# Gated mix of an SSM and a two-layer feed-forward: the narrow tail blocks of both layers are regrouped, and two x tiles are loaded earlier

## The chip, the cores and the metric

The kernel runs on one core of a Trainium2 chip, as one launch. The metric is the device time in microseconds of an execution; 214.89 us is the median of six executions of the kernel before (214.46 to 215.27). All times below are microseconds unless marked ns.

## The reference

For 2048 tokens of width 640, one input x goes through two branches, and a gate of each token mixes them. Cut to what matters:

```
g = sigmoid((x * gate_w).sum(-1))                 # one number per token

# branch A: a diagonal complex recurrence over the tokens
Bu = einsum("bld,pd->blp", x, B_bar)              # 640 -> 640 complex
for t in range(L):  h = Lam_bar * h + Bu[:, t]
a = 2 * einsum("blp,dp->bld", hseq, Cmat).real + x * Dskip

# branch B: feed-forward
h = gelu(x @ w1 + b1)                             # 640 -> 1728
b = h @ w2 + b2                                   # 1728 -> 640

out = g * a + (1 - g) * b
```

The width 1728 is 13 blocks of 128 and a last one of 64. The 64 are what is called the tail here: in the first layer they are 64 output columns, in the second layer 64 rows of the sum.

## The kernel before

**Tiling.** Tokens are taken in four quarters of 512 (index q), each of two SSM blocks of 256 (b) and four chunks of 128 (c). xT[q] holds x transposed, features on partitions. For each quarter:

- `m1(q)` (L633): 13 blocks of the first layer, five matmuls of 512 tokens each (L640), gelu by ScalarE into Gl[q % 2] (L647).
- `bproj(q)` (L672): the projection to the recurrence's input, real and imaginary, ten blocks of five matmuls (L680); ScalarE moves them to U (L689).
- `ssm(b)` (L694): VectorE alone. It rotates U (pre), scans along the tokens (L720, scan), and rotates back (post) into H[b % 3], reading and writing the tiles V and W on the way.
- `gates(q)` (L593): VectorE sums x * gate_w from the untransposed tile xn[q % 2] (L597), ScalarE takes tanh (L604), VectorE makes the factors g and 1 - g.

Output is made by chunks of 128 tokens in `outs` (L872). `m2_prime` (L747) has ScalarE write the bias b2 into two banks of PSUM, one for each half of the 640 columns (L754). `m2_main` (L758) adds 13 matmuls to each half (L767). `m2_tails` (L774) adds the 64 tail rows (L781): for the first half they are read from partitions 0 to 63, for the second from 64 to 127, so the two matmuls use two row tiles of the array, and the gelu values of the tail and W2's tail rows have to stand in both halves of the partitions. `m2_out` (L788) has ScalarE scale the sum by 1 - g into E1 (L795). `cproj` (L802) makes branch A's output from H and CT, 20 matmuls over two banks (L815), which ScalarE scales by g into E2 (L826). `comb` (L830) has VectorE compute xg = x * g * Dskip (L834) and add xg, E1 and E2 (two additions through the helper at L481) into osb, which SP stores (L868). E1, E2, osb and H have three buffers each, xg and xn two. For the last chunk, VectorE adds the second half straight out of PSUM (L848).

The first layer's tail, `m1_tail(q)` (L651), takes two quarters at once: ten matmuls of 64 columns each, alternately on the two column halves of the array, into the lower and upper 64 partitions of one bank (L658). Four gelus follow (L667), since the result of each quarter is written twice, to partitions 0 to 63 and to 64 to 127 of the last block of Gl.

**The order of the work.** There are eight banks of PSUM, given out in turn by `next_bank` (L589) as the program is written. Each operation is declared with what it reads and writes, a length in a cost model and a priority; a list planner (L43) then fixes the order on each engine before the program is emitted. TensorE's priority is the order of declaration, so its queue follows the program's text where the model finds the operands ready. On ScalarE evictions of outputs (5) come before the bias writes (8), and these before gelus and U (10). On VectorE the combination (-50) comes before everything else of the steady state, xg is at 90 + 20q, and pre, scan and post of block b at 100, 101 and 102 + 10b. SP issues the loads by the numbers at their calls: the x tile of quarter 1 at 32, W2 and b2 at 33 to 34.4, the transposed C at 36 and 37, dsk at 38, the second xn at 38.2, and the x tiles of quarters 2 and 3 last, at 39 and 40 (L579, L580). POOL loads the later xn tiles (`xnload`) when the chunks that use the old ones are through.

The text of the order is at L883 to L911. The first tail group, `m1_tail(0)`, comes after m1(1); the second, `m1_tail(2)`, after m1(3). The chunks go through `outs` in groups of 2, 2, 2, 2, 3, 3 and 2, each group with one `m2_tails`, and within a chunk cproj follows m2 directly.

Of the kernel before, what the change touches and what calls it, by code (L numbers as in the profile page):

```python
# [9 lines left out]
BF16 = mybir.dt.bfloat16  # L10
I32 = mybir.dt.int32
ACT = mybir.ActivationFunctionType
# [135 lines left out]
class Prog:  # L148
# [8 lines left out]
    def op(self, name, eng, dur, reads, writes, fn, prio=None, lat=0.0, after=()):  # L157
        deps = {}
        for k in reads:
            for w in self.last_w.get(k, ()):  # L160
                deps[w.idx] = w
        for k in writes:
            for w in self.last_w.get(k, ()):
                deps[w.idx] = w
            for r in self.last_r.get(k, ()):
                deps[r.idx] = r
        for a in after:
            deps[a.idx] = a
        deps = list(deps.values())
        E = self.E  # L170

        def run(eg, deps=deps, eng=eng, fn=fn):
            E.wait(eng, *[d.done for d in deps if not (eng == "pe" and d.eng == "pe")])
            return fn()

        it = self.sch.add(name, eng, dur, deps, run, prio=prio, lat=lat)
        for k in writes:
            self.last_w[k] = [it]
            self.last_r[k] = []
        for k in reads:  # L180
            self.last_r.setdefault(k, []).append(it)
        return it


def bass_gated_mix__ssm_conv_s5__dense_activation_gelu__prompt_kernel(
# [18 lines left out]
    _, S, D = A_x.shape  # L204
# [3 lines left out]
    KD = D // 128  # L208
    KP = P // 128
    NQ = S // 512  # L210
    NCH = S // 128
    T = 256
    NB = S // T
    NF = (F + 127) // 128
    FL = F - (NF - 1) * 128
    assert FL <= 64
    HALF = D // 2
# [8 lines left out]
    with ExitStack() as es:  # L226

        def SB(name, shape, dt):
            return es.enter_context(nc.sbuf_tensor(name, list(shape), dt))
# [4 lines left out]
        W2sb = SB("W2sb", [128, NF, D], BF16)  # L234
        BT = SB("BT", [128, 2, KD, P], BF16)
        CT = SB("CT", [128, 2, KP, D], BF16)
        Gl = [SB(f"Gl_{i}", [128, NF, 512], BF16) for i in range(2)]
        dsk = SB("dsk", [128, D], BF16)
        gwb = SB("gwb", [128, D], BF16)
        b2b = SB("b2b", [128, D], BF16)  # L240
# [3 lines left out]
        b1col = cols[:, 3 * KP:3 * KP + NF]  # L244
# [42 lines left out]
        PS = [es.enter_context(nc.psum_tensor(f"ps{i}", [128, 512], FP32)) for i in range(8)]  # L287
# [13 lines left out]
        op = pr.op  # L301

        def inc(eng, ins):
            return E.inc(eng, ins, eng + "_s")

        def dma_inc(eng, ins, sem):
            SEM(sem)
            E.count.setdefault(sem, 0)
            ins.then_inc(sems[sem], 16)
            E.count[sem] += 16  # L310
            return (sem, E.count[sem])

        def d_act(n):
            return 0.26 + n * 0.00084
# [4 lines left out]
        def d_mm(n):  # L319
            return n / 2400.0 + 0.004  # L320


        def load(name, eng, sem, dst, src, writes, prio, dur=0.5, lat=2.5, reads=(), **kw):
            def fn():
                return dma_inc(eng, engines[eng].dma_start(dst, src), sem)  # L325
            return op(name, eng, dur, reads, writes, fn, prio=prio, lat=lat)
# [18 lines left out]
        def xtrans(q, ks, prio, dur):  # L345
            load_T(f"xT{q}_{ks[0]}", f"l_xT{q}_{ks[0]}", [(xT[q][:, ks[0]:ks[-1] + 1, :], x2[q * 512:(q + 1) * 512, ks[0] * 128:(ks[-1] + 1) * 128])],
                   [("xT", q, k) for k in ks], prio, dur)
# [57 lines left out]
        for i, (k, c0, c1) in enumerate(((0, 0, 2), (0, 2, 4), (1, 0, 4))):  # L405
            bank = 7 - i
# [169 lines left out]
            load_T(f"C{ci}", f"l_C{ci}", [(CT[:, ci, :, :], src)], [("CT", ci)], prio=36 + ci, dur=4.1)  # L576
        load("dsk", "sp", "l_dsk", dsk[:, :], A_Dskip.partition_broadcast(128), ["dsk"], prio=38)
        xnload(1, "sp", prio=38.2)
        xtrans(2, range(KD), 39, 3.4)  # L579
        xtrans(3, range(KD), 40, 3.4)  # L580

        ctr = {"bank": 0, "pe": 0}

        def pe_prio():
            ctr["pe"] += 1
            return ctr["pe"]


        def next_bank():  # L589
            ctr["bank"] += 1  # L590
            return (ctr["bank"] - 1) % 8
# [41 lines left out]
        def m1(q, j0=0):  # L633
            for jf in range(j0, NF - 1):
# [13 lines left out]

                op(f"ge_{q}_{jf}", "act", d_act(512), [("bank", bank), "b1col"], [("gl", q % 2, jf)], f_ge, prio=10)

        def m1_tail(q):  # L651
            bank = next_bank()

            def f_mm():
                t = None
                for k in range(KD):
                    for i in range(2):
                        t = nc.tensor.matmul(PS[bank][64 * i:64 * i + FL, :], W1sb[:, k, nmain:F], xT[q + i][:, k, :],  # L658
                                             start=(k == 0), stop=(k == KD - 1))
                return inc("pe", t)  # L660

            op(f"m1t_{q}", "pe", KD * d_mm(512) + 0.25, XT[q] + XT[q + 1] + [("w1", "r", 1)], [("bank", bank)], f_mm, prio=pe_prio())
            for i in range(2):
                for u in range(2):

                    def f_ge(i=i, u=u):
                        return inc("act", nc.scalar.activation(Gl[i][64 * u:64 * u + FL, NF - 1, :], PS[bank][64 * i:64 * i + FL, :], ACT.Gelu_apprx_tanh,  # L667
                                                               bias=b1col[64 * i:64 * i + FL, NF - 1:NF]))

                    op(f"get_{q}_{i}{u}", "act", d_act(512), [("bank", bank), "b1col"], [("gt", i, u)], f_ge, prio=10)  # L670

        def bproj(q):  # L672
            for ci in range(2):
# [71 lines left out]
        mbank = {}  # L745
# [28 lines left out]
        def m2_tails(cs):  # L774
            def f_mm():
                t = None
                for c in cs:
                    q, t4 = c // 4, c % 4
                    for hf in range(2):
                        r = slice(64 * hf, 64 * hf + FL)  # L780
                        t = nc.tensor.matmul(PS[mbank[c, hf]][:, 0:HALF], Gl[q % 2][r, NF - 1, t4 * 128:(t4 + 1) * 128],  # L781
                                             W2sb[r, NF - 1, hf * HALF:(hf + 1) * HALF], start=False, stop=False, skip_group_check=True)
                return inc("pe", t)

            op(f"m2t_{cs[0]}", "pe", len(cs) * d_mm(HALF) + 0.2, [("gt", c // 4 % 2, u) for c in cs for u in range(2)] + ["w2b", "w2c"],
               [("bank", mbank[c, hf]) for c in cs for hf in range(2)], f_mm, prio=pe_prio())

        def m2_out(c):  # L788
# [13 lines left out]
        def cproj(c):  # L802
            q, b, s = c // 4, c // 2, c % 2
            for hf in range(2):
                bank = next_bank()
                cbank[hf] = bank
                cols = CCOLS[hf] if c == NCH - 1 else slice(hf * HALF, (hf + 1) * HALF)
                n = cols.stop - cols.start

                def f_mm(bank=bank, cols=cols, n=n):  # L810
                    t = None
                    i = 0
                    for ci in range(2):
                        for k in range(KP):
                            t = nc.tensor.matmul(PS[bank][:, 0:n], H[b % NHB][:, ci, k, s * 128:(s + 1) * 128], CT[:, ci, k, cols],  # L815
                                                 start=(i == 0), stop=(i == 2 * KP - 1))
                            i += 1
                    return inc("pe", t)

                op(f"c_{c}_{hf}", "pe", 2 * KP * d_mm(n), [("H", b % NHB), ("CT", 0), ("CT", 1)], [("bank", bank)], f_mm, prio=pe_prio())  # L820

                if c == NCH - 1:
                    continue

                def f_ev(bank=bank, cols=cols):
                    return inc("act", nc.scalar.activation(E2[c % NE][:, cols], PS[bank][:, 0:HALF], ACT.Copy, scale=gcol[:, c:c + 1]))  # L826

                op(f"e2_{c}_{hf}", "act", d_act(HALF), [("bank", bank), ("g", q)], [("E2", c % NE, hf)], f_ev, prio=5)
# [40 lines left out]

            op(f"st{c}", "sp", 0.5, [("osb", c % NO, 0), ("osb", c % NO, 1)], [], f_st, prio=1000 + c, lat=2.5)  # L870

        def outs(*cs):  # L872
            for c in cs:
                m2_prime(c)
            for c in cs:
                m2_main(c)
                if c == cs[0]:
                    m2_tails(cs)
                m2_out(c)
                cproj(c)  # L880
                comb(c)

        m1_first()  # L883
        m1(0, NW)
# [1 line left out]
        ssm(0)  # L886
        gates(0)
        m1(1)
        m1_tail(0)
        ssm(1)  # L890
        bproj(1)
        ssm(2)
        gates(1)
        outs(0, 1)
        outs(2, 3)
        for q in range(2, NQ):
            ssm(2 * q - 1)
            bproj(q)
            ssm(2 * q)
            m1(q)  # L900
            if q % 2 == 1:
                m1_tail(q - 1)
            xnload(q, "pool")
            gates(q)
            if q < NQ - 1:
                outs(4 * q - 4, 4 * q - 3)
                outs(4 * q - 2, 4 * q - 1)
        outs(NCH - 8, NCH - 7, NCH - 6)
        ssm(2 * NQ - 1)
        outs(NCH - 5, NCH - 4, NCH - 3)  # L910
        outs(NCH - 2, NCH - 1)  # L911

        order = pr.sch.order()
        ptr = {e: 0 for e in order}
# [57 lines left out]
```

## Time and profile before

| What | Value |
|---|---|
| Median of six runs | 214.89 (214.46 to 215.27) |
| The profiled execution | 214.74 |
| Its span, first to last instruction | 213.4 |
| Granted TensorE clock | 1.00 |
| TensorE on the chain that ended last, from / to | 7.71 / 211.31 |
| L767, second layer: 416 matmuls of 128x320 | 59.1 busy |
| L781, its tails: 32 matmuls on 64 rows | 3.4 busy |
| L658, first layer's tails: 20 matmuls on 64 columns | 2.5 busy |
| L667, gelus of the tails: 8 | 5.5 busy, 683 ns each |
| L754, bias into PSUM: 32 | 14.1 busy, 441 ns each |

A page of the profile gives the busy time of each engine (PE is TensorE's matmuls, PEld its weight loads, which run beside them, DVE VectorE, ACT ScalarE, SP the queue that issues DMAs), the chain of work that ended last, and groups of instructions by line. Neighbouring matmuls overlap in the array and their ends are modelled, so the busy times of single groups of matmuls add up to more or less than the time they take; the chain in order of time is better for that, since it counts each stretch once. An idle time is shown with what ended it, as in [1.37 <-ACT E L826]: 1.37 us, ended by ScalarE's write at line 826.

### The profile page before, as it was taken

To read this page: it belongs to the slowest core of one execution; us is meant where nothing else is said; L and a number is where in the kernel's file an instruction comes from. 1 tells how busy PE (TensorE), PEld (TensorE's weight loads), DVE (VectorE), ACT (ScalarE), POOL (GpSimd) and SP (SyncE) were. 2 spreads that over 40 slices of the span, in tenths; PEclk is the share of its full clock that TensorE was granted. 3 is DMA by queue.
4 is the path that set the end of the run, shared out by engine and by line. 5 is a ranking of instruction groups with operands and counts; after the bars stand their busy time and mean duration, and the time that the engine had idled before them with its cause. 6 is when DMAs were issued, how large, how long until landed. Compare 5 with 4: busy or idle time off the path is not lost.

```text
span 213.4 us, 3114 instructions
## 1 busy us (share of the span) xinstructions
PE 209.9 (98%) x1264; PEld 119.7 (56%) x1264; DVE 188.7 (88%) x262; ACT 113.3 (53%) x205; POOL 2.5 (1%) x10
## 2 busy tenths in 40 slices
PE   8999999999999999999999999999999999999996
PEld 3344444444567675444467767444446777677673
DVE  2499999999899999999999959999999998988712
ACT  2489556679554234557835332556786554535230
POOL 1000000000000010000000010000000000000000
DMA  5999899698000040000000013000000010001000
GB/s 145 309 261 196 218 383 202 159 235 141 0 0 34 31 125 31 31 0 0 0 3 0 31 45 144 15 16 0 3 0 2 0 34 31 31 3 61 31 34 31
DMA packets 31114, 16.08 MB, mean 75 GB/s; under 512 B 22908, under 2 KB 30332, under 8 KB 31100
## 3 DMA queue, kind: packets, MB, share of 16 engines
q1 hardware_dynamic: 30752, 14.57, 27.4%
q0 software_dynamic: 288, 1.31, 2.0%
q8 instruction: 10, 0.16, 0.3%
q14 instruction: 4, 0.03, 0.0%
q10 hardware_dynamic: 60, 0.01, 0.0%
HBM read 7.63 MB, written 2.62 MB: 48 GB/s over the span
## 4 chain that ended last, share of the span: by engine, by line
PE 95%; DMA 2%; ACTq 1%; POOL 0%; issue 0%; DVE 0%; POOLq 0%
PE ps L767 27%; PE ps L640 22%; PE ps L815 21%; PE ps L680 20%; PE ps L620 3%; DMA rows<-in_B_b_dram 2%; PE ps L781 1%; PE ps L658 1%; ACTq L325 1%; DVE osb L848 0%; POOL io_i L381 0%; PE ps L431 0%; POOL rows L371 0%; POOL st_i L383 0%; POOL st_i L382 0%
## 5 line engine op out<-in xcount | busy, mean ns | idle before, releaser
L767 PE MATMUL ps<-W2sb,Gl 128*128 128x320 bf16 x416 | 59.1, 299 | 0.0
L767 PEld LDWEIGHTS ps<-W2sb,Gl 128*128 128x128 bf16 x416 | 40.6, 98 | 16.5 <-ACT Gl L647 0.4
L640 PE MATMUL ps<-xT,W1sb 128*128 128x512 bf16 x220 | 48.1, 379 | 0.0
L815 PE MATMUL ps<-CT,H 128*128 128x320 bf16 (+2 forms) x320 | 46.1, 299 | 0.0
L720 DVE TENSOR_TENSOR_SCAN W<-atab,V 128x1280 bf16<-128x1280 f32 x16 | 44.3, 2812 | 0.3
L680 PE MATMUL ps<-xT,BT 128*128 128x512 bf16 x200 | 43.8, 379 | 0.0
L815 PEld LDWEIGHTS ps<-CT,H 128*128 128x128 bf16 x320 | 30.7, 98 | 13.5 <-issue 1.6
L795 ACT ACTIVATE E<-ps,g1col 128x320 bf16<-128x320 f32 x32 | 16.1, 526 | 40.5 <-PE ps L781 21.5
L640 PEld LDWEIGHTS ps<-xT,W1sb 128*128 128x128 bf16 x220 | 21.5, 98 | 26.0
L647 ACT ACTIVATE Gl<-ps,cols 128x512 bf16<-128x512 f32 x44 | 29.7, 690 | 11.5 <-PE ps L640 11.5
L680 PEld LDWEIGHTS ps<-xT,BT 128*128 128x128 bf16 x200 | 19.5, 98 | 23.4 <-ACT Gl L647 0.4
L689 ACT ACTIVATE U<-ps 128x512 bf16<-128x512 f32 x40 | 23.6, 595 | 15.7 <-PE ps L680 15.7
L826 ACT ACTIVATE E<-ps,gcol 128x320 bf16<-128x320 f32 x30 | 15.8, 528 | 17.9 <-PE ps L815 17.9
L754 ACT ACTIVATE ps<-b2b 128x320 f32<-128x320 bf16 x32 | 14.1, 441 | 1.0
L834 DVE SCALAR_TENSOR_TENSOR xg<-xn,gcol,dsk 128x640 bf16<-128x640 bf16 x16 | 13.8, 882 | 0.3
L481 DVE TENSOR_TENSOR osb<-xg,E 128x640 bf16<-128x640 bf16 x15 | 7.3, 486 | 7.7 <-ACT E L826 7.6
L597 DVE SCALAR_TENSOR_TENSOR scr<-xn,gwb 128x640 bf16<-128x640 bf16 x16 | 13.2, 823 | 0.4
L481 DVE TENSOR_TENSOR V<-V,W 128x1280 bf16<-128x1280 bf16 x16 | 12.5, 822 | 0.3
L481 DVE TENSOR_TENSOR H<-H,V 128x1280 bf16<-128x1280 bf16 x16 | 12.5, 822 | 0.3
L481 DVE TENSOR_TENSOR V<-mr,U 128x2560 bf16<-128x2560 bf16 x8 | 11.9, 1489 | 0.2
L481 DVE TENSOR_TENSOR H<-c,W 128x2560 bf16<-128x2560 bf16 x8 | 11.9, 1488 | 0.1
L481 DVE TENSOR_TENSOR V<-s,W 128x2560 bf16<-128x2560 bf16 x8 | 11.9, 1485 | 0.0
(79 smaller groups left out, 102.1 us busy)
## 6 DMA issues: line engine op xcount, KB each, us to landing
out_dram<-osb SPq DMA_DIRECT2D x15, 160.0 KB, 1.8
W2sb<-in_B_w_dram SPq DMA_DIRECT2D x1, 2080.0 KB, 11.1
xn<-in_A_x_dram POOLq DMA_DIRECT2D x2, 640.0 KB, 4.7
W1sb<-in_B_w_dram SPq DMA_DIRECT2D x4, 256.0 KB, 4.1
xn<-in_A_x_dram SPq DMA_DIRECT2D x1, 640.0 KB, 7.5
W1sb<-in_B_w_dram SPq DMA_DIRECT2D x1, 480.0 KB, 4.8
W1sb<-in_B_w_dram SPq DMA_DIRECT2D x1, 400.0 KB, 5.6
xn<-in_A_x_dram SPq DMA_DIRECT2D x1, 384.0 KB, 5.6
```

Source lines behind the costliest of these rows:

```text
L481: return inc("dve", nc.vector.tensor_tensor(out=o, in0=a, in1=b, op=o_))
L640: t = nc.tensor.matmul(PS[bank][:, :], W1sb[:, k, jf * 128:(jf + 1) * 128], xT[q][:, k, :], start=(k == 0), stop=(k == KD - 1))
L647: return inc("act", nc.scalar.activation(Gl[q % 2][:, jf, :], PS[bank][:, :], ACT.Gelu_apprx_tanh, bias=b1col[:, jf:jf + 1]))
L680: t = nc.tensor.matmul(PS[bank][:, :], BT[:, ci, kd, k * 128:(k + 1) * 128], xT[q][:, kd, :], start=(kd == 0), stop=(kd == KD - 1))
L689: return inc("act", nc.scalar.activation(dst, src, ACT.Copy, scale=1.0 if ci == 0 else -1.0))
L720: t = inc("dve", nc.vector.tensor_tensor_scan(out=g[:, ci, :], data0=a, data1=v[:, ci, :], initial=0.0, op0=ALU.mult, op1=ALU.add))
L754: return inc("act", nc.scalar.activation(PS[bank][:, 0:HALF], b2b[:, cols], ACT.Copy))
L767: t = nc.tensor.matmul(PS[bank][:, 0:HALF], Gl[q % 2][:, jf, t4 * 128:(t4 + 1) * 128], W2sb[:, jf, cols], start=False, stop=False, skip_gr ...
L795: return inc("act", nc.scalar.activation(E1[c % NE][:, cols], PS[bank][:, 0:HALF], ACT.Copy, scale=g1col[:, c:c + 1]))
L815: t = nc.tensor.matmul(PS[bank][:, 0:n], H[b % NHB][:, ci, k, s * 128:(s + 1) * 128], CT[:, ci, k, cols], start=(i == 0), stop=(i == 2 * K ...
L826: return inc("act", nc.scalar.activation(E2[c % NE][:, cols], PS[bank][:, 0:HALF], ACT.Copy, scale=gcol[:, c:c + 1]))
L834: return inc("dve", nc.vector.scalar_tensor_tensor(out=xg[c % 2][:, :], in0=xn[q % 2][:, c % 4, :], scalar=gcol[:, c:c + 1], in1=dsk[:, :] ...
```

## The change

1. The gelu values of the tail leave Gl and get four tiles of their own, Gt, one per quarter. ScalarE writes each once, to partitions 0 to 63; a DMA on SP copies it to partitions 64 to 127.
2. Both calls of `m1_tail` stand together after m1(1), so the tails of all tokens are made there, from the x tiles of all four quarters.
3. The x tiles of quarters 2 and 3 move in SP's order from the end of the loads to a place before W2 (priorities 32.6 and 32.7).
4. `outs` takes the four chunks of a quarter as one group: eight banks are primed with the bias, one `m2_tails` of eight matmuls follows the first chunk's m2, and cproj and comb of a chunk come after the m2 of the next one. The last block's `ssm` is declared inside the third group, after chunk 9's cproj, which is the last reader of the H buffer that it writes.

```diff
-        Gl = [SB(f"Gl_{i}", [128, NF, 512], BF16) for i in range(2)]
+        Gl = [SB(f"Gl_{i}", [128, NF - 1, 512], BF16) for i in range(2)]
+        Gt = [SB(f"Gt_{i}", [128, 512], BF16) for i in range(NQ)]
...
-        xtrans(2, range(KD), 39, 3.4)
-        xtrans(3, range(KD), 40, 3.4)
+        xtrans(2, range(KD), 32.6, 3.4)
+        xtrans(3, range(KD), 32.7, 3.4)
...
             for i in range(2):
-                for u in range(2):
-
-                    def f_ge(i=i, u=u):
-                        return inc("act", nc.scalar.activation(Gl[i][64 * u:64 * u + FL, NF - 1, :], PS[bank][64 * i:64 * i + FL, :], ACT.Gelu_apprx_tanh,
-                                                               bias=b1col[64 * i:64 * i + FL, NF - 1:NF]))
-
-                    op(f"get_{q}_{i}{u}", "act", d_act(512), [("bank", bank), "b1col"], [("gt", i, u)], f_ge, prio=10)
+
+                def f_ge(i=i):
+                    return inc("act", nc.scalar.activation(Gt[q + i][0:FL, :], PS[bank][64 * i:64 * i + FL, :], ACT.Gelu_apprx_tanh,
+                                                           bias=b1col[64 * i:64 * i + FL, NF - 1:NF]))
+
+                op(f"get_{q}_{i}", "act", d_act(512), [("bank", bank), "b1col"], [("gt", q + i, 0)], f_ge, prio=10)
+                load(f"gt{q + i}", "sp", f"l_gt{q + i}", Gt[q + i][64:64 + FL, :], Gt[q + i][0:FL, :], [("gt", q + i, 1)], 500, lat=2.5, reads=[("gt", q + i, 0)])
...
-                        t = nc.tensor.matmul(PS[mbank[c, hf]][:, 0:HALF], Gl[q % 2][r, NF - 1, t4 * 128:(t4 + 1) * 128],
+                        t = nc.tensor.matmul(PS[mbank[c, hf]][:, 0:HALF], Gt[q][r, t4 * 128:(t4 + 1) * 128],
...
-        def outs(*cs):
+        def outs(q, mid=None):
+            cs = range(4 * q, 4 * q + 4)
             for c in cs:
                 m2_prime(c)
             for c in cs:
                 m2_main(c)
                 if c == cs[0]:
                     m2_tails(cs)
                 m2_out(c)
-                cproj(c)
-                comb(c)
+                if c > cs[0]:
+                    cproj(c - 1)
+                    comb(c - 1)
+                    if mid is not None and c == cs[0] + 2:
+                        mid()
+            cproj(cs[-1])
+            comb(cs[-1])
...
-        m1_tail(0)
+        for q in range(0, NQ, 2):
+            m1_tail(q)
         ssm(1)
         bproj(1)
         ssm(2)
         gates(1)
-        outs(0, 1)
-        outs(2, 3)
+        outs(0)
         for q in range(2, NQ):
...
             m1(q)
-            if q % 2 == 1:
-                m1_tail(q - 1)
             xnload(q, "pool")
             gates(q)
             if q < NQ - 1:
-                outs(4 * q - 4, 4 * q - 3)
-                outs(4 * q - 2, 4 * q - 1)
-        outs(NCH - 8, NCH - 7, NCH - 6)
-        ssm(2 * NQ - 1)
-        outs(NCH - 5, NCH - 4, NCH - 3)
-        outs(NCH - 2, NCH - 1)
+                outs(q - 1)
+        outs(NQ - 2, mid=lambda: ssm(2 * NQ - 1))
+        outs(NQ - 1)
```

More of the change, by code (lines that the diff above doesn't have):

```diff
@@ L649, in m1 @@
                 op(f"ge_{q}_{jf}", "act", d_act(512), [("bank", bank), "b1col"], [("gl", q % 2, jf)], f_ge, prio=10)
+        tbank = {}
         def m1_tail(q):
             bank = next_bank()
+            tbank[q] = bank
             def f_mm():
@@ L780, in f_mm @@
                         r = slice(64 * hf, 64 * hf + FL)
-                        t = nc.tensor.matmul(PS[mbank[c, hf]][:, 0:HALF], Gl[q % 2][r, NF - 1, t4 * 128:(t4 + 1) * 128],
+                        t = nc.tensor.matmul(PS[mbank[c, hf]][:, 0:HALF], Gt[q][r, t4 * 128:(t4 + 1) * 128],
                                              W2sb[r, NF - 1, hf * HALF:(hf + 1) * HALF], start=False, stop=False, skip_group_check=True)
                 return inc("pe", t)
-            op(f"m2t_{cs[0]}", "pe", len(cs) * d_mm(HALF) + 0.2, [("gt", c // 4 % 2, u) for c in cs for u in range(2)] + ["w2b", "w2c"],
+            op(f"m2t_{cs[0]}", "pe", len(cs) * d_mm(HALF) + 0.2, [("gt", c // 4, u) for c in cs for u in range(2)] + ["w2b", "w2c"],
                [("bank", mbank[c, hf]) for c in cs for hf in range(2)], f_mm, prio=pe_prio())
```

## The prediction

> **What bounds the kernel now.** I read the page first: busy times, then the chain that ended last by line.
>
> ```profile
> PE 209.9 (98%) x1264; PEld 119.7 (56%) x1264; DVE 188.7 (88%) x262; ACT 113.3 (53%) x205; POOL 2.5 (1%) x10
> PE 95%; DMA 2%; ACTq 1%; POOL 0%; issue 0%; DVE 0%; POOLq 0%
> ```
>
> TensorE is 95% of the chain, and from 7.71 us to 211.31 nothing else is on it. So time is gained only by taking away TensorE time, and lost only by making TensorE wait. The chain in order of time shows what its pieces cost (start, length, line, matmuls):
>
> ```profile
> 44.62 1.20 PE ps L658 x10
> 45.82 10.90 PE ps L680 x50
> 56.72 3.53 PE ps L767 x26
> 60.25 0.38 PE ps L781 x4
> 60.63 2.82 PE ps L815 x20
> 63.45 3.53 PE ps L767 x26
> 66.98 2.72 PE ps L815 x20
> ...
> 82.68 10.79 PE ps L680 x50
> 93.47 14.03 PE ps L640 x65
> ...
> 159.48 3.64 PE ps L767 x26
> 163.12 0.51 PE ps L781 x6
> ```
>
> Two things are to be seen. The dense pieces follow each other with no gap: 26 matmuls of L767 take 3.53, 136 ns each. And each change between whole-array and tiled matmuls costs about 0.1 us: the piece right after a tiled one is longer than its like (L815 2.82 against 2.72, L680 10.90 against 10.79, L767 3.64 against 3.53).
>
> **Second layer's tails (L781).** Four matmuls take 0.38, six 0.51: a pair on two row tiles adds 0.13, which leaves 0.12 of entry, and 0.10 goes into the piece behind. Before there are five groups of four and two of six: 5 x 0.48 + 2 x 0.61 = 3.62. After there are four groups of eight. That size is not in the trace; one more pair on six gives 0.64, with the exit 0.74, so 4 x 0.74 = 2.96. Saved 0.66. If the two pairs beyond four did not overlap (two matmuls at 136 ns, 0.27 a pair) a group would be 0.28 dearer, 1.1 in all, and the saving gone; the six-matmul row speaks against this, and I take 0.66. On the other side, 16 pairs with no entry or exit at all would take 2.1 and save 1.5, but all seven groups of the trace show that price.
>
> **First layer's tails (L658).** Ten column-tiled matmuls take 1.20, that is five pairs of 0.216 (L640: 14.03 / 65) and 0.12 of entry; the exit is 0.11. Two groups cost 2 x 1.31 = 2.62. Adjacent they cost 1.20 + 5 x 0.216 + 0.11 = 2.39: saved 0.23, or nothing if the second group pays an entry again (the trace has no two such groups in a row). I take 0.23, as the tiling does not change between them. The gelus of the tails go from eight to four (683 ns each), ScalarE time that no matmul waits for: the four at 159.5 are followed by an idle 1.34 us.
>
> **The sum.** 0.66 + 0.23 = 0.89. Written as a timeline of TensorE: both first-layer tails end at 46.90, bproj(1) at 57.80, outs(0) at 83.54 (four m2 of 3.53, tails 0.74, four cproj of 2.72: 25.74), block 2 at 108.36, outs(1) 134.10, block 3 at 158.92, outs(2) 184.66, outs(3) 210.40. Before, it ends at 211.31. The profiled run took 214.74, 1.34 more than its span; with 0.9 off it is 213.84. The median of the runs is 214.89, 0.15 above the profiled run, so I forecast 213.99, say 214.0.
>
> **The copies by DMA.** Four new transfers of 64 KB, SBUF to SBUF, on SP's queue. No such row exists; the nearest is the last store of 64 KB, 1.5 us to landing, the slowest ordinary transfer of all 11.1. SP is issuing loads until 50.56 and the gelus are done about 49, so the first copy is issued at about 50.6 and landed between 52 and 61.7; the first second-layer tails come at 61.33. Taken: 1.5 plus some queueing, hidden by about 8 us; at the far bound 0.4 us of stall, once. Behind the four waiting copies in SP's queue are only the stores, the first at 66.65 before and about 70 after.
>
> **The x tiles, sooner.** Two transposes move ahead of W2's three loads, b2, both C transposes, dsk and the second xn on SP.
>
> ```profile
> 17.40 3.58 SPq L332 DMA_TRANSPOSE xT<-in_A_x_dram  x1
> ...
> 22.12 4.78 SPq L325 DMA_DIRECT2D W2sb<-in_B_w_dram  x3
> ...
> 39.62 10.94 SPq L332 DMA_TRANSPOSE xT<-in_A_x_dram  x2
> ```
>
> The two hold SP for 7.2 (twice the first row) to 10.94 us (the last); all else is later by that, and the queue ends near 50.6 as now. Worst case: the x tiles are issued by 33.1 and landed (up to 10.9) by 44, needed at 45.7. With the rows' times from issue to landing, W2 is there by 22.1 + 10.9 + 11.1 = 44.1 (needed at 57.8); b2, issued at 26.95 before, by 26.95 + 10.9 + 7.1 = 45 (first bias write at about 51); the second C, at 34.80, by 34.8 + 10.9 + 5.7 = 51.4 (65.6); dsk, at 38.52, by 38.5 + 10.9 + 6.4 = 55.8 (57.75); the second xn, at 39.14, by 57.5 (its gates at 90.6). Everything has cover; the thinnest is dsk, whose wait would hold VectorE's queue, with the scan behind it, but H of block 1 is ready at 71.9 and now first read at 78.1. So this edit costs nothing, and gains nothing by itself. On POOL the xn loads wait for xg3 and xg7, a few us later; the gates that read them run at 133 and 172.
>
> **Cproj one chunk later.** No instruction is added. H, E2 and the stores get 3 to 5 us more room at most chunks. E1's three buffers get less: e1 of chunk c waits for the combination of c-3, which now ends some 10 us before instead of 16; VectorE's longest block is a scan of 5.5, so it holds. Cproj(c) takes the banks of its own m2, so e1 must be out of them: 0.6 us is needed, 2.7 there for a group's last chunk, 6.2 for the others.
>
> **A rule that speaks against it.** All eight banks must hold the bias before the eight tails start. Row first:
>
> ```profile
> 50.37 0.44 ACT L754 ACTIVATE ps<-b2b 128x320 f32<-128x320 bf16 x1
> 50.74 0.58 ACT L689 ACTIVATE U<-ps 128x512 bf16<-128x512 f32 x1
> ```
>
> ScalarE interleaves bias writes with evictions while TensorE still fills other banks: 0.44 + 0.58 = 1.02 us per bank, where TensorE takes 1.08 (L680: 10.79 / 10). It keeps up; only the last bank's eviction and bias (0.6 + 0.44, with gelu 0.7 + 0.44 and a backlog under 1) remain when m2 starts, and m2's 26 matmuls cover 3.53. The Trainium skill (TensorEngine Tiling (Array Packing), Gotcha 1: PSUM Pressure) says that row tiling raises the pressure on PSUM, different row tiles writing different banks[...]. Taken at its strongest, eight bias writes after the last eviction, it gives 0.6 + 8 x 0.44 = 4.1, a stall of 0.6 in each of four groups: 214.0 + 2.4 = 216.4. The row decides for no stall.
>
> **Rivals.**
> 1. *Pressure on the banks*, as just worked out: 216.4; 0.22 us per group eats the gain. Against it: ScalarE is busy 53%, and the bank order leaves most bias writes early. Chance 0.07.
> 2. *H of the last block is late*, so slower than before. VectorE's queue is written out ahead, and it already idles for a combination that the plan put before the last block's work:
>
> ```profile
> 192.67 0.49 DVE L481 TENSOR_TENSOR osb<-xg,E 128x640 bf16<-128x640 bf16 x1 [1.37 <-ACT E L826]
> ...
> 195.20 1.48 DVE L481 TENSOR_TENSOR H<-c,W 128x2560 bf16<-128x2560 bf16 x1
> ```
>
>  From 195.20 H takes 4.48 us; cproj(14), its first reader, starts at 204.96 after, so H may start up to 200.48. If the plan keeps chunk 12's combination (now possible at 196) ahead of it, with two xg (1.67), H starts at 198.7 and is in time. If chunk 13's too (possible at 202.0), H is ready at 208.4: TensorE waits 3.4, and the end is 217.4. It decides from a start at 201.4. Chance 0.10.
> 3. *Nothing to measure*: extra pairs or the joined first-layer group pay a switch after all, or late loads take back half: 214.5 to 215.3. Chance 0.16.
>
> **How the numbers follow.** Forecast (213.7 to 214.4): 0.67. A measurement here tells about 0.2% (0.43 us) from no change, so the gain of 0.9 is twice that. Faster 0.67; same 0.16; slower 0.17 (rivals 1 and 2). Range 213.6 to 215.7: it holds the forecast and rival 3, the chance of a short stall, and leaves out most of rivals 1 and 2.
>
> **What would show it.** Right: four L781 pieces of about 0.64 with eight matmuls; one L658 piece of twenty, about 2.3; L767 and L815 at 3.53 and 2.72 elsewhere; TensorE ending at 210.4. Wrong: idle time before L781 released by ScalarE (rival 1), before L815 released by VectorE (rival 2), before L658 by DMA (x tiles late), or L781 of 0.8 and more.

## The result and the profile after

The changed kernel takes 213.75 us (median of 18 runs, 213.41 to 214.51); the kernel before, measured beside it, 214.75 (39 runs). The ratio is 0.9955, with a 95% interval of 0.9947 to 0.9963: 0.97 us gained (0.8 to 1.1), where 0.9 was forecast.

The chain of the changed kernel, in order of time (start, length, line, matmuls). The lines have moved by one to five: L662 is the first layer's tails, L771 m2, L785 its tails, L819 cproj, L684 bproj, L641 m1.

```profile
44.81 2.28 PE ps L662 x20
47.09 10.90 PE ps L684 x50
57.98 3.53 PE ps L771 x26
61.52 0.65 PE ps L785 x8
62.17 3.64 PE ps L771 x26
65.81 2.72 PE ps L819 x20
68.52 3.53 PE ps L771 x26
72.05 2.72 PE ps L819 x20
74.77 3.53 PE ps L771 x26
78.30 5.43 PE ps L819 x40
83.73 10.79 PE ps L684 x50
...
201.66 3.53 PE ps L771 x26
205.19 5.45 PE ps L819 x40
```

One piece of 20 column-tiled matmuls stands where two of ten were, and takes 2.28. The four tail pieces hold eight matmuls and take 0.65; the 3.64 behind each is 0.11 over the 3.53 of the other m2 pieces. There is no gap. From the start of the first tail piece to the end of TensorE's work, the stretch that the change touches, the time is now 210.64 - 44.81 = 165.83; before it was 211.31 - 44.62 = 166.69. So 0.86 came out of this stretch.

The busy times by engine say that work stayed as it was, save for ScalarE's four gelus:

```profile
PE 209.0 (98%) x1264; PEld 120.3 (57%) x1264; DVE 188.9 (89%) x262; ACT 111.3 (52%) x201; POOL 2.5 (1%) x10
```

That stretch is a sharper measure than the median here. Ahead of it lies the same work in every kernel of this study, yet in the profiles of the nine kernels below the first tail piece begins anywhere from 44.17 to 44.81; from there on, kernels with the same groups agree to 0.01 (one profile of each). The scatter comes from the start: in eight of the nine the chain passes through a small load of rows that takes 4.43 to 4.94 (before 4.75, changed kernel 4.94), and the first tail piece begins 37.26, to 0.01, after it has landed. In the ninth, e7, the chain passes through another load; from the last 31 matmuls of L621 (L620 before) to the tails it takes 36.91, as before. So nothing that the change does shows in the time ahead of the stretch. The next table has it for every kernel whose TensorE never stopped, beside the ratio of the runs.

| Kernel | Stretch, us | Against the changed kernel | Ratio to before (interval) |
|---|---|---|---|
| before | 166.69 | +0.86 | 1 |
| changed | 165.83 | 0 | 0.9955 (0.9947 to 0.9963) |
| e1: first-layer tails apart | 166.06 | +0.23 | 0.9969 (0.9959 to 0.9978) |
| e2: tails of two chunks | 166.68 | +0.85 | 1.0002 (0.9995 to 1.0010) |
| e3: tails of one chunk | 168.38 | +2.55 | 1.0071 (1.0056 to 1.0085) |
| e4: first-layer part alone | 166.46 | +0.63 | 0.9991 (0.9981 to 1.0001) |
| e6: cproj not delayed | 165.83 | 0.00 | 0.9961 (0.9947 to 0.9975) |
| e7: gelu twice, no copies | 165.83 | 0.00 | 0.9957 (0.9944 to 0.9971) |
| e8: gate first | 165.84 | +0.01 | 0.9967 (0.9956 to 0.9978) |

### The profile page after: what moved, and what is told of

Same layout as the page of the kernel before. It is cut to its first block, busy times and chain, and to the rows that moved or that the text cites. A ratio compares the mean times of both kernels' runs of the same rounds, so it can differ in the third digit from the quotient of the medians.

```text
span 212.8 us, 3123 instructions
## 1 busy us (share of the span) xinstructions
PE 209.0 (98%) x1264; PEld 120.3 (57%) x1264; DVE 188.9 (89%) x262; ACT 111.3 (52%) x201; POOL 2.5 (1%) x10
## 4 chain that ended last, share of the span: by engine, by line
PE 95%; DMA 2%; ACTq 1%; POOL 0%; issue 0%; DVE 0%; POOLq 0%
PE ps L771 27%; PE ps L641 22%; PE ps L819 20%; PE ps L684 20%; PE ps L621 3%; DMA rows<-in_B_b_dram 2%; PE ps L785 1%; PE ps L662 1%; ACTq L326 1%; DVE osb L852 0%; POOL io_i L382 0%; PE ps L432 0%; POOL rows L372 0%; POOL st_i L384 0%; POOL st_i L383 0%
## 5 line engine op out<-in xcount | busy, mean ns | idle before, releaser
L771 PE MATMUL ps<-W2sb,Gl 128*128 128x320 bf16 x416 | 59.2, 299 | 0.0
L771 PEld LDWEIGHTS ps<-W2sb,Gl 128*128 128x128 bf16 x416 | 40.4, 98 | 17.0 <-issue 1.1
L641 PE MATMUL ps<-xT,W1sb 128*128 128x512 bf16 x220 | 48.1, 379 | 0.0
L819 PE MATMUL ps<-CT,H 128*128 128x320 bf16 (+2 forms) x320 | 45.4, 299 | 0.0
L684 PE MATMUL ps<-xT,BT 128*128 128x512 bf16 x200 | 43.8, 379 | 0.0
L819 PEld LDWEIGHTS ps<-CT,H 128*128 128x128 bf16 x320 | 31.3, 98 | 12.2
L641 PEld LDWEIGHTS ps<-xT,W1sb 128*128 128x128 bf16 x220 | 21.5, 98 | 26.0
L684 PEld LDWEIGHTS ps<-xT,BT 128*128 128x128 bf16 x200 | 19.5, 98 | 23.4 <-ACT Gt L670 0.4
```

Source lines behind the costliest of these rows:

```text
L641: t = nc.tensor.matmul(PS[bank][:, :], W1sb[:, k, jf * 128:(jf + 1) * 128], xT[q][:, k, :], start=(k == 0), stop=(k == KD - 1))
L684: t = nc.tensor.matmul(PS[bank][:, :], BT[:, ci, kd, k * 128:(k + 1) * 128], xT[q][:, kd, :], start=(kd == 0), stop=(kd == KD - 1))
L771: t = nc.tensor.matmul(PS[bank][:, 0:HALF], Gl[q % 2][:, jf, t4 * 128:(t4 + 1) * 128], W2sb[:, jf, cols], start=False, stop=False, skip_gr ...
```

## The experiments

The theory: TensorE pays a fixed price for each change between whole-array and tiled matmuls, and the change saves it by making fewer groups. The rivals: the gain is from cproj's later place, from loading x sooner, or from ScalarE's saved gelus.

**e1: the first layer's tails apart again.**

```diff
-        for q in range(0, NQ, 2):
-            m1_tail(q)
+        m1_tail(0)
...
             m1(q)
+            if q == 2:
+                m1_tail(2)
```

> The changed kernel, but the second group of the first layer's tails is made after m1(2) instead of next to the first group. Theory (TensorE pays about 0.23 for each group, entry and exit): two L662 pieces of 1.20 instead of one of 2.28, 0.23 later than the changed kernel, so 213.75 + 0.23 = 214.0 and a ratio to before of about 0.9966. Rival (joining is worth nothing, the gain is all in the second layer's tails or in the order): no difference from the changed kernel, 0.9955.

Measured: 213.94, ratio 0.9969. By the runs alone this can't be told from the changed kernel; the chain tells it. Its two first-layer pieces, and what follows the second:

```profile
44.54 1.20 PE ps L662 x10
...
107.21 1.20 PE ps L662 x10
108.41 3.64 PE ps L771 x26
```

Two pieces of 1.20 are 2.40 instead of 2.28, and the m2 behind the second has the exit, 3.64 instead of 3.53: 0.23 in all, which is what the stretch is longer by. Joining is worth 0.23.

**e2 and e3: smaller groups in the second layer.**

```diff
-                if c == cs[0]:
-                    m2_tails(cs)
+                if (c - cs[0]) % 2 == 0:
+                    m2_tails((c, c + 1))
```

> The changed kernel, but the second layer's tails go in groups of two chunks (four matmuls) instead of four. Everything else stays: one quarter per call, eight banks primed, cproj one chunk later. Theory (price per group): eight groups of 0.38 + 0.10 are 3.84, against 4 x (0.65 + 0.11) = 3.04 measured after the change, so 0.8 later, about 214.55, ratio 0.9992. Rival (the gain comes from cproj's later place or the room it gives to other engines, not from the number of groups): unchanged, 213.75.

In e3 the two lines became one, `m2_tails((c,))`.

> The changed kernel with one tail group per chunk: sixteen groups of two matmuls. Theory (a fixed price per group of 0.12 + 0.10 and 0.13 per pair): 16 x 0.35 = 5.6 against 3.04, so 2.56 later: 216.3, ratio 1.0074. If the price is not fixed but grows with the matmuls that a group holds, the sixteen small groups are cheaper than that: with 3.04 / 16 = 0.19 a pair the time would be unchanged.

Measured: e2 214.62, level with the kernel before (ratio 1.0002); e3 216.21, ratio 1.0071. From the chain of e3, the first two tail groups:

```profile
57.66 3.53 PE ps L771 x26
61.19 0.24 PE ps L785 x2
61.43 3.64 PE ps L771 x26
65.07 0.24 PE ps L785 x2
65.31 2.82 PE ps L819 x20
```

A group of two takes 0.24, of four 0.38, of six 0.51, of eight 0.65: 0.136 per pair and 0.105 for the entry, at every size, and then 0.10 to 0.11 in the piece behind, whichever line that is. A change of line between two whole-array pieces costs nothing: L771 and L819 take 3.53 and 2.72 behind each other. With that, e2 should lose 4 x 0.21 = 0.84 and e3 12 x 0.21 = 2.5; the stretches are 0.85 and 2.55 longer. The price is per group, not per matmul. e2 has everything else of the change, the later cproj too, so cproj's place gains nothing.

**e4: the first-layer part alone.** The changed kernel with the old text of the output:

```diff
-        def outs(q, mid=None):
-            cs = range(4 * q, 4 * q + 4)
+        def outs(*cs):
...
-                if c > cs[0]:
-                    cproj(c - 1)
-                    comb(c - 1)
...
+                cproj(c)
+                comb(c)
...
-        outs(0)
+        outs(0, 1)
+        outs(2, 3)
```

> The kernel before with only the first-layer part of the change: own tiles for the tails, copied by DMA, both tail groups together, x tiles loaded sooner; the output chunks go in the old groups with cproj right behind m2. Theory: the seven old groups of second-layer tails stay, so only the 0.23 of the joined group is gained: ratio to before 0.9989. Rival (loading x sooner, or ScalarE's four gelus saved, is worth something by itself): more than 0.4 gained, ratio under 0.998.

Measured: 214.35, ratio 0.9991. The stretch is 0.23 shorter than before, just what joining is worth by e1; the rival's 0.998 lies just outside the interval (0.9981 to 1.0001), and the stretch is far from the 0.4 that it asked for. So the early x tiles, the copies by DMA and the four gelus saved bring nothing of their own. The two parts add up: 0.23 here and 0.63 for the second layer are the 0.86.

**e5: the x tiles late again.**

```diff
-        xtrans(2, range(KD), 32.6, 3.4)
-        xtrans(3, range(KD), 32.7, 3.4)
+        xtrans(2, range(KD), 39, 3.4)
+        xtrans(3, range(KD), 40, 3.4)
```

> The changed kernel with the two x tiles back at the end of SP's loads. TensorE's order stays the same. Theory (the early load gains nothing by itself but is what the joined first-layer tails need): before the change the last x tile was issued at 47.0 and landed at 52.6, while the second tail group asks for it at 45.9, so TensorE stands still for about 6.7 and the time is 220.4. If the idle stretch also costs clock, as the Trainium skill (TensorE: Matmul & The Clock Gate, Part 1) says of pauses over 3.4 us, the matmuls after it run at half speed for about 3.4 us and it is 222. Rival (the transfer is hidden anyway): 213.75.

Measured: 223.33, ratio 1.0400 (1.0373 to 1.0426), more than any of the three numbers. TensorE's timeline around the two halves of the first-layer tails, with the idle time in brackets:

```profile
44.25 1.27 PE L662 MATMUL ps<-xT,W1sb 128*64 128x512 bf16 x10
53.26 2.34 PE L662 MATMUL ps<-xT,W1sb 128*64 128x512 bf16 x10 [7.74 <-issue]
```

And the busy times in stretches of 2 us; PEclk is the granted clock of TensorE:

```profile
46.00:48.00 2.00, 0.00 (x0) 0.00 (x0) 1.97 (x3) 0.93 (x2) 0.00 (x0) 1.00 1.04 176
48.00:50.00 2.00, 0.00 (x0) 0.00 (x0) 1.97 (x5) 0.00 (x0) 0.00 (x0) 0.82 1.05 223
50.00:52.00 2.00, 0.00 (x0) 0.00 (x0) 1.93 (x5) 0.00 (x0) 0.00 (x0) 0.50 1.17 220
52.00:54.00 2.00, 0.74 (x4) 0.42 (x6) 1.97 (x4) 0.00 (x0) 0.00 (x0) 0.50 0.61 131
54.00:56.00 2.00, 2.00 (x10) 0.61 (x7) 1.97 (x3) 0.36 (x1) 0.00 (x0) 0.50 0.04 8
56.00:58.00 2.00, 2.00 (x11) 0.89 (x10) 1.93 (x3) 1.60 (x3) 0.00 (x0) 0.97 0.13 33
```

The clock (the third number from the end) falls to a half within the pause and comes back after work resumes: the mean of 0.82 in 48 to 50 puts the fall at 49.3, 3.8 into the pause, and the 0.97 in 56 to 58 puts the return at 56.1, 2.8 after the restart. The second half of the tails then takes 2.34, instead of the 1.08 by which twenty matmuls are longer than ten, and bproj(1) behind it 11.17 instead of 10.90, as the chain has it:

```profile
53.26 2.34 PE ps L662 x10
55.60 11.17 PE ps L684 x50
```

The loss is 7.74 of standing still and 1.26 + 0.27 at half clock, 9.3. The stretch says the same, 175.18 and so 9.35 longer; the medians of e5 and the changed kernel are 9.6 apart. My expectation had the pause 1.0 too short: the last x tile landed at 53.1 instead of 52.6, and TensorE ran out of work at 45.5 instead of 45.9. The Trainium skill (TensorE: Matmul & The Clock Gate, Part 1) gives windows of about 3.4 us, one for the falling and one for the coming back. An estimate from that page, 3.4 us at half speed, is a loss of 1.7; here it was 1.5. So the early load gains nothing by itself and is what the joined group can't do without.

**e6: cproj not delayed.**

```diff
-                if c > cs[0]:
-                    cproj(c - 1)
-                    comb(c - 1)
-                    if mid is not None and c == cs[0] + 2:
-                        mid()
-            cproj(cs[-1])
-            comb(cs[-1])
+                cproj(c)
+                comb(c)
+                if mid is not None and c == cs[0] + 1:
+                    mid()
```

> The changed kernel, but cproj and comb of a chunk are declared right after its own m2, not after the next one's. Groups of tails as in the changed kernel. The planner then puts at least half of the next m2 between the tails and the first cproj, 13 matmuls or 1.78 us, and e1 needs 0.05 + 2 x 0.53 = 1.1 to clear the banks. Theory (the later cproj is no gain of its own, only cover for e1): within 0.2 of 213.75 where the planner's filler covers e1; the first quarter is the risk, since e1 of chunk 0 waited for the gate until 63.6 after the change. Rival (the later cproj is itself part of the gain): 0.4 or more lost.

Measured: 213.79, ratio 0.9961, and the stretch is the same to 0.01. Its chain at the tails of the first and the second quarter:

```profile
61.28 0.65 PE ps L785 x8
61.93 3.64 PE ps L771 x26
65.57 5.43 PE ps L819 x40
...
111.85 0.65 PE ps L785 x8
112.50 1.87 PE ps L771 x13
114.38 2.72 PE ps L819 x20
```

The planner by itself put half of the next m2 (in the first quarter all of it) between the tails and the first cproj. So the text's new order is not needed for the gain. Whether cproj could follow the eight tails with no other work between them was not tried.

**e7: the gelu twice, without the copies.**

```diff
...
-                op(f"get_{q}_{i}", "act", d_act(512), [("bank", bank), "b1col"], [("gt", q + i, 0)], f_ge, prio=10)
-                load(f"gt{q + i}", "sp", f"l_gt{q + i}", Gt[q + i][64:64 + FL, :], Gt[q + i][0:FL, :], [("gt", q + i, 1)], 500, lat=2.5, reads=[("gt", q + i, 0)])
+                for u in range(2):
...
+                        return inc("act", nc.scalar.activation(Gt[q + i][64 * u:64 * u + FL, :], PS[bank][64 * i:64 * i + FL, :], ACT.Gelu_apprx_tanh,
...
+                    op(f"get_{q}_{i}{u}", "act", d_act(512), [("bank", bank), "b1col"], [("gt", q + i, u)], f_ge, prio=10)
```

> The changed kernel, but ScalarE writes each tail twice (eight gelus, all after the joined group) and the four copies by DMA are gone. Theory: ScalarE gets 2.8 us more just before bproj(1), so the bias writes of the first quarter end about 2.3 later, at 61.4, where TensorE starts the tails at 61.5: no stall or at most some tenths, 213.75 to 214.1. Rival (the copies are what makes the joined group possible): the tails of the first quarter wait over 1 us for ScalarE, 214.8 or more. If the copies themselves cost time, this kernel is faster than the changed one.

Measured: 213.64, ratio 0.9957, stretch the same. ScalarE's timeline, from the eight gelus to the last bias write of the first quarter (this kernel's lines are one further on from L672):

```profile
45.41 5.63 ACT L672 ACTIVATE Gt<-ps,cols 64x512 bf16<-64x512 f32 x8 [0.52 <-PE ps L662]
51.07 1.57 ACT L694 ACTIVATE U<-ps 128x512 bf16<-128x512 f32 x3
52.74 0.44 ACT L759 ACTIVATE ps<-b2b 128x320 f32<-128x320 bf16 x1
...
59.65 0.44 ACT L759 ACTIVATE ps<-b2b 128x320 f32<-128x320 bf16 x1
```

The eight gelus hold ScalarE for 5.63 and it catches up, since a bank's eviction and bias take it 0.98 in a row where TensorE fills one in 1.08: the last bias write ends at 60.09, and TensorE starts the tails at 60.88. In the changed kernel 2.4 us are between them (59.09 and 61.52). The copies buy room that is not used.

**e8: the gate first.**

```diff
-            op(f"gth{q}", "act", 0.25, [("gz", q)], [("gth", q)], fn2, prio=50)
+            op(f"gth{q}", "act", 0.25, [("gz", q)], [("gth", q)], fn2, prio=4)
```

> The changed kernel with the tanh of the gate put ahead of bias writes and gelus on ScalarE, so that VectorE's plan can make the gate factors before the scan of block 1. In the changed kernel e1 of chunk 0 waited 4.5 us for them, and cproj(0) needs e1's banks 1.1 us after e1 got through. Theory (TensorE was not reached by that wait): the wait goes, the time stays at 213.75 within 0.1. Rival (the wait was close enough to cost TensorE something): faster by up to 0.2.

Measured: 213.97, ratio 0.9967, the stretch 165.84. In the changed kernel ScalarE shows this:

```profile
58.65 0.44 ACT L758 ACTIVATE ps<-b2b 128x320 f32<-128x320 bf16 x1
59.03 0.19 ACT L605 ACTIVATE gth<-gz 128x4 f32<-128x4 f32 x1
63.75 1.36 ACT L799 ACTIVATE E<-ps,g1col 128x320 bf16<-128x320 f32 x3 [4.53 <-DVE g1col L610]
```

and in e8 the same three places are

```profile
58.62 0.44 ACT L758 ACTIVATE ps<-b2b 128x320 f32<-128x320 bf16 x1
62.17 0.95 ACT L799 ACTIVATE E<-ps,g1col 128x320 bf16<-128x320 f32 x2 [3.12 <-PE ps L785]
64.04 0.53 ACT L799 ACTIVATE E<-ps,g1col 128x320 bf16<-128x320 f32 x1 [0.92 <-PE ps L771]
```

The wait for the gate is gone, ScalarE is ready 1.6 sooner, and TensorE ends at the same point of its stretch. The idle 4.53 was off the path.

## Why the prediction was right

**The mechanism and the sum.** Both halves are shown: 0.23 for the first layer (forecast 0.23), 0.63 for the second (forecast 0.66). As a stretch, 165.78 was forecast (210.40 - 44.62) and 165.83 measured; that TensorE ended at 210.64 and not at 210.40 is mostly its start, 0.19 later. The small difference is in the terms: eight tails take 0.65 and not 0.64, their exit into an m2 is 0.11 and not the 0.10 that it was into a cproj. The stretch gives 0.86; the medians give 0.97 with an interval (0.8 to 1.1) that holds it. The 0.1 between them needs no second cause.

**The bound from both sides.** The dear end, two extra pairs at 0.27 each, is refuted by 0.136 a pair at all four sizes. A second entry between adjacent groups of the same tiling is not paid: 20 matmuls take 2.28, that is 1.20 and five more pairs of 0.216.

**The x tiles.** Costing the move at nothing held. The two transposes took SP 8.50, between the bounds of 7.2 and 10.94, and everything moved past was in time. SP was through with the loads at 46.9, nearer the lower bound than the 50.6 of the forecast. What the edit is for was said only by its due time, "needed at 45.7"; e5 shows the price when that is missed, 9.6.

**The copies by DMA.** Here the nearest row was the wrong one. I took 1.5 from a store at the quiet end of the kernel; the four copies took 5.0 to 6.8 from issue to landing:

```profile
L326 SPq DMA_DIRECT2D Gt<-Gt x4: 509/594/1172, 47.0 to 49.4; - x4
...
DMA to landing us min/median/max: 5.0/6.0/6.8
```

They were issued right behind the 640 KB of xn, which landed at 53.7. The last copy landed at 54.4, 7.1 ahead of the first use. The cover was a little smaller than the "about 8" and still enough; e7 without copies shows that nothing hung on it.

**Cproj one chunk later.** "No instruction is added", no gain and no loss: e2 and e6 agree. One case was left out of the room for e1: a group's first chunk has the 3.64 of the next m2, neither 2.7 nor 6.2, and its two halves leave their banks one after the other once the tails are through, which takes 1.0 (112.74 to 113.73 in the second quarter) and not 0.6. It fitted.

**Rival 1, pressure on the banks.** It did not happen; the last of eight bias writes ends 2.3 to 2.5 before the tails start, in all four quarters. e7, with 2.8 more on ScalarE just ahead, still had 0.8 left. The row weighed against the rule, 1.02 a bank against 1.08, was the right one to read.

**Rival 2, H of the last block late.** The forecast had the plan keep chunk 12's combination ahead of H, with a start at 198.7; it went the other way. In the changed kernel post starts at 192.20, after chunk 11's combination and one xg, and chunk 12's combination comes behind it, at 196.60. VectorE's timeline:

```profile
191.40 0.89 DVE L838 SCALAR_TENSOR_TENSOR xg<-xn,gcol,dsk 128x640 bf16<-128x640 bf16 x1
192.20 1.49 DVE L482 TENSOR_TENSOR H<-c,W 128x2560 bf16<-128x2560 bf16 x1
...
195.12 1.56 DVE L482 TENSOR_TENSOR H<-H,V 128x1280 bf16<-128x1280 bf16 x2
196.60 0.48 DVE L482 TENSOR_TENSOR osb<-xg,E 128x640 bf16<-128x640 bf16 x1
...
202.26 0.49 DVE L482 TENSOR_TENSOR osb<-xg,E 128x640 bf16<-128x640 bf16 x1 [3.73 <-ACT E L830]
```

H is ready at 196.68 and first read at 205.19, where the last piece of L819 (chunks 14 and 15) starts: 8.5 us of room, where before it was 2.6 (199.68 and 202.23). Chunk 12's cproj ended only at 195.41, so at 192.20 its combination could not be done; the planner took post. That H came so early was not foreseen.

**Not foreseen.** The forecast named dsk as the thinnest cover on VectorE's queue. What came nearest to the path of the waits read here was another thing: eight bias writes instead of four stand before the gate's tanh on ScalarE (59.03 instead of 57.25), and VectorE's plan puts the gate's factors behind the scan of block 1. They come at 63.65 instead of 57.71, and cproj(0), at 65.81, needs the banks that this e1 clears at about 64.7. The gain stood 1.1 us from a first loss.

## What to carry to other kernels

When one engine is the whole chain, count its changes of mode as well as its instructions: here each group of tiled matmuls costs 0.21 to 0.23 beside its matmuls, whatever it holds, so the fewest and fullest groups are best. The rest of the change gained nothing by itself; the early load was needed for one of the groups. Work that is gathered early needs its inputs early, and a load made late is paid for twice, by the pause and by the slower clock after it. For differences under half a per cent, measure the stretch that the change touches on the chain: here four kernels with the same groups agree in it to 0.01 us, while the runs of the changed kernel scatter by 1.1.

## What the runs showed of the hardware that was not expected

- The price of entering a tiled group is close for row tiles (0.105 at L785, 64 rows) and column tiles (0.12 at L662, 64 columns), and so is that of leaving (0.10 to 0.11), into whichever line comes next. The weight loads (PEld) of the changed kernel show what is different there:

```profile
61.45 0.39 PEld L785 LDWEIGHTS ps<-W2sb,Gt 64*128 64x128 bf16 x8 [0.26 <-issue]
62.09 3.38 PEld L771 LDWEIGHTS ps<-W2sb,Gl 128*128 128x128 bf16 x26 [0.26 <-issue]
65.51 0.51 PEld L819 LDWEIGHTS ps<-CT,H 128*128 128x128 bf16 x4
```

  Between whole-array pieces the first load begins 0.30 ahead of its piece (65.51 and 65.81); into and out of the tails only 0.07 and 0.08 ahead (61.45 and 61.52, 62.09 and 62.17). One load takes 0.094 at L785, 0.110 at L662 and 0.098 at L771, so each price is about one load that is no longer hidden. This fits the numbers; no run here tests it.
- A copy of 64 KB within SBUF took 5.0 to 6.8 us when issued behind the second C, dsk and the 640 KB of xn. In e1 the two copies issued near 109 us, with no load ahead of them, took 1.9 each, and in e5 the four took 1.9 to 2.4. So the time lay in what stood ahead of the copies.
- SP's time to issue the same DMA changed with its place in the order: W2's three loads held SP for 4.78 before and 2.04 after, the first transpose of C for 7.18 and 8.60. What decides it was not tested.
